# Both batches of a kv head as one unit in a decode attention block

## The chip, the cores and the metric

The kernel runs on one core of a Trainium2 chip. Five engines work side by side, each in the order of its own instructions: TensorE (PE) multiplies matrices into PSUM, VectorE (DVE), ScalarE (ACT) and GpSimd (POOL) work on elements, and SyncE (SP) issues here all transfers between device memory and SBUF. The metric is the time of one execution in device microseconds, as the median of some runs; a profile is taken of one execution of its own.

## The reference

A decode step for two sequences (B = 2, one token each): adaptive layer norm, attention over the last 4096 cached positions with 32 query heads on 8 kv heads (4 query heads share one), then a feed-forward layer, each with a gate and a residual.

```python
mod = (silu(c) @ w_mod).reshape(2, 6, 1, 512)       # shift, scale, gate, twice
h = layernorm(x) * (1 + ca) + sa
q = h @ wq                                          # 512 -> 32 heads x 128
scores = q . k[last 4096] * 128 ** -0.5             # per batch and kv head: 4 x 4096
o = softmax(scores) @ v[last 4096]
x = x + ga * (o @ wo)                               # 4096 -> 512
h = layernorm(x) * (1 + cb) + sb
out = x + gb * (silu(h @ w1) @ w2)                  # 512 -> 1792 -> 512
```

All is float32. The keys and values of the 16 pairs of kv head and batch are 2 MB each, 64 MB in all; the weights are some 30 MB.

## The kernel before, in words

**Transfers.** All big loads go through one ring of eight tiles of 128 x 4096 floats (`RING`, lines 20, 55 and 69), issued by SP in the order in which the program asks for them: `w_mod`, `wq`, keys and values, `wo`, `w1`, `w2`. A new tile takes the slot that is released first in program order, and its transfer is issued when the last reader of that slot is done. `fetch(t)` (L341) asks for the keys of step t and the values of step t-1, so that keys and values alternate.

**Steps.** A step t is one pair of kv head and batch (`seq`, L337). Keys arrive with 32 consecutive positions on each partition. `keys` (L348) turns a quarter of a key tile with VectorE's transpose of 32 x 32 blocks, so that four transposes of 128 x 1024 make `kT`. `scores` (L363) multiplies with the query, spread over a block pattern of 32 columns (`qbd`): four products over j are summed, each for four column groups cc of the array, and group cc takes the 256 columns of quarter cc of the keys. So the scores of a step are 128 x 256: four groups of 32 rows. Each float32 product is two records in the profile (two passes).

**Softmax.** `maxima` (L376) takes the maximum of each row; a product with the identity (L460) turns the 128 maxima into a row `mT`; `maxrow` (L381) reduces it to one value per query head (`mg`) and spreads it again (`mrow`); `exponentials` (L395) turns `mrow` into a bias by a product with `negscale` (`bp`, L398) and computes exponentials with the row sums. `turn` (L411) transposes them (`xp`) and spreads them over a mask (`zp`); `permute` (L423) multiplies by a small identity (`pT`) and copies the result to `ptb`.

**Values.** `weighted` (L306) multiplies the probabilities with the value tile in eight products of 512 columns, on four column groups, in two halves, and copies the sum to `ob` (L322). `collect` (L325) sums it into `o_all`, which holds the outputs of all heads for one batch in 32 rows per column group.

**Order.** The loop at L436 writes the order out by hand, and `keep_in_program_order` binds each engine to it. In iteration t VectorE turns half of the keys of t, does `maxrow` of t-1, turns the other half, does `turn` of t-1; TensorE does the scores of t, collects t-2, permutes and weights t-1. After the loop come the row sums (`rx`, `lp`, `rl`, L484 to L501), the normalisation (`on`), a product that spreads heads (`oq`, `oTn`, L505 to L512), the output product (`acc_o`, L530, and `ao`, L539), the second norm and the feed-forward layer (`hid` L570, `uT` L602, `acc_yw` L604, `acc_y` L614).

Of the kernel before, what the change touches and what calls it, by code (L numbers as in the profile page):

```python
# [13 lines left out]
P = 128  # L14
# [9 lines left out]
def adaln_block(  # L24
# [80 lines left out]
    for t, src in ((c_ch, c), (x_ch, x2)):  # L105
# [25 lines left out]
    selg = const([P, G], "selg")  # L131
    nc.vector.tensor_reduce(
        selg, id4[:, 0:16].rearrange("p (i g) -> p g i", g=G), axis=AX.X, op=ALU.add
    )

# [42 lines left out]
    rowsum = const([P, HKV, B], "rowsum")  # L178
# [48 lines left out]
    for k in range(4):  # L227
# [8 lines left out]
        if k == 0:  # L236
            mean_a, rstd_a = moments(x_ch, "a")
            xn = once.tile([P, P], F32, tag="xs", name="xn_a")
# [6 lines left out]
    h_a = once.tile([P, P], F32, tag="h", name="h_a")  # L245
# [56 lines left out]
    o_all = bank("O", "o_all")[:, : B * DH].rearrange("p (b d) -> p b d", b=B)  # L302

    o_ps = {}

    def weighted(t, vt, part):  # L306


        if part == 0:
            o_ps[t] = bank("D", f"o{t}")  # L310
        for c in range(4):
            n = 4 * part + c
            inorder(nc.tensor.matmul(  # L313
                o_ps[t][32 * c : 32 * c + 32, :],
                ptb[t % 2][:, 16 * n : 16 * n + 32],
                vt[:, 512 * n : 512 * n + 512],
                start=(part == 0),
                stop=(part == 1),
            ))
        if part == 1:  # L320
            sb_ = once.tile([P, 4 * DH], F32, tag="wide", name=f"ob{t}")
            inorder(nc.scalar.copy(sb_, o_ps[t]))  # L322
            return sb_

    def collect(t, b, h, o_sb):  # L325

        for m in range(4):
            inorder(nc.tensor.matmul(  # L328
                o_all[32 * m : 32 * m + 32, b, :],
                selh[:, m, HQ - G - G * h : 2 * HQ - G - G * h],  # L330
                o_sb[:, m * DH : (m + 1) * DH],
                start=(t == 0),
                stop=(t == NP - 1),
                skip_group_check=True,
            ))

    seq = [(h, b) for h in range(HKV) for b in range(B)]  # L337
    NP = len(seq)
    kt, vt, wot, kT = {}, {}, [], {}

    def fetch(t):  # L341

        if t < NP:
# [313 lines left out]
```

## Time and profile before

| | |
|---|---|
| median of 3 runs | 238.27 us (238.16 to 239.41) |
| the profiled execution | 237.98 us, span 236.2 us |
| transfers | 97.75 MB, mean 414 GB/s, queue 1 busy for 97.1% of the span |
| PE | 160.8 us busy (68%), 1476 products |
| PEld (weight loads) | 61.9 us (26%) |
| DVE | 118.3 us (50%), 212 instructions |
| ACT | 35.2 us (15%) |
| POOL | 9.3 us (4%) |
| mean granted clock of TensorE | 0.848 |

A row of a group names line, engine, operation, what it writes and reads, shapes and count; then its busy time, the mean of one in ns, and the idle time of its engine before it with what ended it. A row of the timeline or of the chain begins with its start in us from the start of the span and its length. A row of a window gives busy time and number of instructions of PE, PEld, DVE, ACT and POOL, then the granted clock of TensorE, the share of the transfer engines and GB/s. PE's records are pipelined: one record is longer than the distance to the next.

### The profile page before, as it was taken

What the parts mean: (1) busy time and instruction counts of PE and PEld (TensorE: products, weight loads), DVE (VectorE), ACT (ScalarE), POOL (GpSimd) and SP (SyncE); (2) the same over time, 40 slices, a digit from 0 to 9 for tenths busy, and PEclk for the clock granted to TensorE, in tenths of its full rate; (3) what the DMA queues carried; (4) which work ended last, traced back from release to release, by engine and by line L of the source; (5) the groups of instructions that cost most, each with busy time, mean ns of one, the idle gap of its engine ahead of it and who ended that gap; (6) DMA issues with size and microseconds to landing.
All of it is one profiled execution on the core that took longest, in us unless ns stands there. A gap on an engine that the chain in (4) does not pass through costs nothing.

```text
span 236.2 us, 3508 instructions
## 1 busy us (share of the span) xinstructions
PE 160.8 (68%) x1476; PEld 61.9 (26%) x1476; DVE 118.3 (50%) x212; ACT 35.2 (15%) x96; POOL 9.3 (4%) x30
## 2 busy tenths in 40 slices
PE   0193864395978777596876869659768696694843
PEld 0121111121333233231323324324223232223302
DVE  0614000658688947658476594764946742102130
ACT  2300000103022211112011120210211202003210
POOL 8400000100000000000000000000000000000000
PEclk9998577757699997978879797995997978779799
DMA  6999999999999999999999999999999999999990
GB/s 252 424 438 422 438 433 419 433 434 436 416 441 433 416 436 430 438 416 441 427 422 438 426 436 425 441 422 425 434 430 426 430 441 416 433 432 416 425 382 31
DMA packets 7607, 97.75 MB, mean 414 GB/s; under 512 B 920, under 2 KB 936, under 8 KB 1576
## 3 DMA queue, kind: packets, MB, share of 16 engines
q1 hardware_dynamic: 7592, 97.54, 97.1%
q8 instruction: 11, 0.18, 0.3%
q14 instruction: 4, 0.03, 0.0%
HBM read 97.53 MB, written 0.00 MB: 413 GB/s over the span
## 4 chain that ended last, share of the span: by engine, by line
DMA 78%; DVE 14%; PE 5%; SPq 1%; issue 0%; ACT 0%; DVEq 0%
DMA k<-in_A_k_cache_dram 41%; DMA wo<-in_A_wo_dram 15%; DMA wq<-in_A_wq_dram 13%; DVE kT L352 12%; DMA w<-in_B_w_dram 7%; DMA wm<-in_w_mod_dram 3%; PE s L368 3%; PE q L271 2%; SPq L74 1%; PE acc_y L616 0%; DVE qbd L294 0%; DVE mrow L390 0%; DVE mx L378 0%; DVE qT L280 0%; ACT qbd L294 0%
## 5 line engine op out<-in xcount | busy, mean ns | idle before, releaser
L352 DVE STREAM_TRANSPOSE kT<-k 128x1024 f32<-128x1024 f32 x64 | 75.4, 1215 | 17.0 <-DMA k<-in_A_k_cache_dram 16.9
L368 PE MATMUL s<-kT,qbd 128*32 128x256 f32 x512 | 69.2, 512 | 9.0 <-DVE kT L352 8.2
L313 PE MATMUL o<-v,ptb 128*32 128x512 f32 x256 | 35.4, 630 | 5.7 <-ACT ptb L433 5.7
L368 PEld LDWEIGHTS s<-kT,qbd 128*32 128x32 f32 x512 | 23.4, 139 | 46.0 <-DVE kT L352 29.6
L398 PE MATMUL bp<-negscale,mrow 1*128 1x1 f32 x32 | 6.6, 274 | 22.6 <-DVE mrow L390 22.6
L378 DVE TENSOR_REDUCE mx<-s 128x1 f32<-128x256 f32 x16 | 6.8, 424 | 28.7 <-PE s L368 28.7
L271 PE MATMUL q<-wq,hq_T 128*32 128x512 f32 x64 | 12.8, 944 | 9.9 <-DMA wq<-in_A_wq_dram 9.9
L322 ACT COPY ob<-o 128x512 f32<-128x512 f32 x16 | 9.4, 586 | 37.6 <-PE o L313 37.6
L398 PEld LDWEIGHTS bp<-negscale,mrow 1*128 1x128 f32 x32 | 5.3, 205 | 36.4 <-DVE mrow L390 36.4
L433 ACT COPY ptb<-pT 128x128 f32<-128x128 f32 x16 | 4.3, 266 | 64.5 <-PE pT L426 64.5
L328 PE MATMUL o_all<-ob,selh 128*32 128x128 f32 x128 | 12.6, 295 | 1.1 <-ACT ob L322 0.7
L426 PE MATMUL pT<-zp,id 128*32 128x128 f32 x128 | 13.2, 298 | 0.2 <-DVE zp L416 0.2
L280 DVE STREAM_TRANSPOSE qT<-q 128x512 f32<-128x512 f32 x2 | 1.4, 717 | 20.0 <-PE q L271 20.0
L416 DVE TENSOR_TENSOR zp<-xp,group 128x512 f32<-128x512 f32 x16 | 11.1, 692 | 0.5
L313 PEld LDWEIGHTS o<-v,ptb 128*32 128x32 f32 x256 | 7.8, 111 | 11.7 <-ACT ptb L433 10.4
L328 PEld LDWEIGHTS o_all<-ob,selh 128*32 128x32 f32 x128 | 7.5, 124 | 4.4 <-ACT ob L322 2.3
L426 PEld LDWEIGHTS pT<-zp,id 128*32 128x32 f32 x128 | 7.7, 123 | 0.9 <-issue 0.5
L402 ACT ACTIVATE pr<-s,bias 128x256 f32<-128x256 f32 x16 | 7.6, 474 | 0.7 <-ACT bias L400 0.2
L271 PEld LDWEIGHTS q<-wq,hq_T 128*32 128x32 f32 x64 | 2.3, 145 | 19.6 <-DMA wq<-in_A_wq_dram 10.9
L414 DVE STREAM_TRANSPOSE xp<-pr 128x256 f32<-128x256 f32 x16 | 6.4, 397 | 2.2 <-ACT pr L402 2.2
L532 PE MATMUL acc_o<-wo,oTn 128*32 128x512 f32 x48 | 6.9, 735 | 0.4 <-DVE oTn L510 0.4
L203 PE MATMUL mean_a<-mv_a,avg 128*128 128x1 f32 x2 | 0.6, 361 | 9.4 <-DVE mv_a L200 9.4
(126 smaller groups left out, 94.0 us busy)
## 6 DMA issues: line engine op xcount, KB each, us to landing
k<-in_A_k_cache_dram SPq DMA_DIRECT2D x16, 2048.0 KB, 33.9
v<-in_A_v_cache_dram SPq DMA_DIRECT2D x16, 2048.0 KB, 33.0
wq<-in_A_wq_dram SPq DMA_DIRECT2D x4, 2048.0 KB
wo<-in_A_wo_dram SPq DMA_DIRECT2D x4, 2048.0 KB, 35.0
wm<-in_w_mod_dram SPq DMA_DIRECT2D x4, 1536.0 KB, 10.3
w<-in_B_w_dram SPq DMA_DIRECT2D x2, 1024.0 KB, 18.7
w<-in_B_w_dram SPq DMA_DIRECT2D x1, 1792.0 KB
w<-in_B_w_dram SPq DMA_DIRECT2D x2, 896.0 KB
```

The lines of the kernel that those rows point to most:

```text
L271: nc.tensor.matmul(q_ps[n][32 * g : 32 * g + 32, :], hq_T[:, k, :], wv[:, n, g], start=(k == 0), stop=(k == 3),)
L313: inorder(nc.tensor.matmul(o_ps[t][32 * c : 32 * c + 32, :], ptb[t % 2][:, 16 * n : 16 * n + 32], vt[:, 512 * n : 512 * n + 512], start=(p ...
L322: inorder(nc.scalar.copy(sb_, o_ps[t]))
L328: inorder(nc.tensor.matmul(o_all[32 * m : 32 * m + 32, b, :], selh[:, m, HQ - G - G * h : 2 * HQ - G - G * h], o_sb[:, m * DH : (m + 1) * DH],
L352: inorder(nc.vector.transpose(kT[t][:, :, 8 * n4 : 8 * n4 + 8, :].rearrange("p j n k -> p n j k"), kt[t][:, n4 * 1024 : (n4 + 1) * 1024].r ...
L368: inorder(nc.tensor.matmul(s_ps[t][32 * cc : 32 * cc + 32, :], qbd[h // 4][:, h % 4, b, j, :], kT[t][:, j, 8 * cc : 8 * cc + 8, :], start= ...
L378: inorder(nc.vector.tensor_reduce(mx[t], s_ps[t], axis=AX.X, op=ALU.max))
L398: inorder(nc.tensor.matmul(bp[:, 0:1], mrow[t % 2], negscale, start=True, stop=True))
L402: inorder(nc.scalar.activation(pr[t].rearrange("p s k -> p (s k)"), s_ps[t], AF.Exp, bias=bias, scale=SCALE, accum_out=rowsum[:, h, b : b ...
L416: inorder(nc.vector.tensor_mul(zp, xp[:, None, :, 0:16].to_broadcast([P, 4, 8, 16]), group[:, :, None, None].to_broadcast([P, 4, 8, 16]),))
L426: inorder(nc.tensor.matmul(tp[32 * i : 32 * i + 32, :], id4, zp.rearrange("p c s x -> p (c s) x")[:, :, 4 * i : 4 * i + 4], start=True, st ...
L532: nc.tensor.matmul(acc[32 * g : 32 * g + 32, :], oTn[:, q, :], wot[q // 8][:, q % 8, :], start=(q < 4), stop=(q >= 20),)
```

## The change

One unit is now a kv head with both batches. `fetch(h)` asks for two key tiles, then two value tiles. `scores` runs once per batch on two column groups (batch 0 on rows 0 to 63 of the result, batch 1 on rows 64 to 127), each with 512 columns, into one 128 x 512 tile. Row maxima, their exchange, bias, exponentials, `turn` (now with the permutation in it) and the copy of the probabilities run once per head with tiles of twice the size: 128 x 512 scores, 128 x 1024 `zp`, 128 x 256 `pT`. `weighted` sums all sixteen products of both batches into one tile, with the probabilities of the batches kept apart by rows (`ptb` now has 32 columns per product, half of them zero); its copy `ob` and `collect` run once per head, and `collect` writes 64 rows at a time with a `selh` of twice the width. `o_all` is 128 x 128 instead of 128 x 256, and the row sums have one column per head, so that `selg`, `half` and `even` sort the batches apart at the end. Some tiles of the ends share buffers (`xn`, `h_a`, `on`, `aoT`, `hidT`). The order of an iteration is: first quarter of keys of batch 0, `turn` of the head before, the other three quarters, `weighted` of the head before, scores of batch 0, `collect` of the head before, keys and scores of batch 1, maxima and exponentials.

```diff
@@ -128,21 +128,34 @@
         rep4.rearrange("p (a r) -> p a r", a=4), id4[:, None, :].to_broadcast([P, 4, 32])
     )
     group = const([P, 4], "group")
     nc.vector.tensor_reduce(
         group, ident.rearrange("p (a r) -> p a r", r=32), axis=AX.X, op=ALU.add
     )
-    selh = const([P, 4, 2 * HQ - G], "selh")
+    half, even = const([P, B], "half"), const([P, B], "even")
+    nc.vector.tensor_reduce(
+        half, group.rearrange("p (b c) -> p b c", b=B), axis=AX.X, op=ALU.add
+    )
+    nc.vector.tensor_reduce(
+        even, group.rearrange("p (c b) -> p b c", b=B), axis=AX.X, op=ALU.add
+    )
+    selg0, selg = const([P, G], "selg0"), const([P, B, G], "selg")
+    nc.vector.tensor_reduce(
+        selg0, id4[:, 0:16].rearrange("p (i g) -> p g i", g=G), axis=AX.X, op=ALU.add
+    )
+    nc.vector.tensor_mul(
+        selg,
+        selg0[:, None, :].to_broadcast([P, B, G]),
+        half[:, :, None].to_broadcast([P, B, G]),
+    )
+    selh = const([P, 4, HQ - G + 2 * HQ], "selh")
     nc.gpsimd.memset(selh, 0.0)
     nc.vector.tensor_copy(
-        selh[:, :, HQ - G : HQ], id4[:, 0:16].rearrange("p (m g) -> p m g", g=G)
+        selh[:, :, HQ - G :].rearrange("p m (b y) -> p m b y", b=B)[:, :, :, 0:G],
+        id4.rearrange("p (b m g) -> p m b g", b=B, g=G),
     )
     quad = const([P, 4, P], "quad")
...
-    ptb = [const([P, P + 16], f"ptb{i}") for i in range(2)]
+    ptb = [const([P, 17 * 32], f"ptb{i}") for i in range(2)]
-        nc.gpsimd.memset(t[:, P:], 0.0)
+        nc.gpsimd.memset(t, 0.0)
-    rowsum = const([P, HKV, B], "rowsum")
+    rowsum = const([P, HKV], "rowsum")
...
@@ -299,168 +313,158 @@
-    o_all = bank("O", "o_all")[:, : B * DH].rearrange("p (b d) -> p b d", b=B)
...
-    seq = [(h, b) for h in range(HKV) for b in range(B)]
...
+    o_all = bank("O", "o_all")[:, :DH]
+    inorder = tc.keep_in_program_order
     kt, vt, wot, kT = {}, {}, [], {}
...
+    s_ps, mT, pr, o_sb = {}, {}, {}, {}
+    def fetch(h):
+        for b in range(B):
+            kt[h, b] = load_k(b, h)
+        for b in range(B):
+            vt[h, b] = load_v(b, h)
+    def keys(h, b, n4):
         if n4 == 0:
...
+            kT[h, b] = ktp.tile([P, 4, 32, 32], F32, tag="kT", name=f"kT{h}_{b}")
         inorder(nc.vector.transpose(
...
+            kT[h, b][:, :, 8 * n4 : 8 * n4 + 8, :].rearrange("p j n k -> p n j k"),
+            kt[h, b][:, n4 * 1024 : (n4 + 1) * 1024].rearrange("p (n j r) -> p n j r", j=4, r=32),
         ))
...
-        s_ps[t] = bank("A", f"s{t}")[:, :256]
+    def scores(h, b):
+        if b == 0:
+            s_ps[h] = bank("A", f"s{h}")
         for j in range(4):
...
+            for c in range(2):
+                r = 64 * b + 32 * c
                 inorder(nc.tensor.matmul(
...
+                    s_ps[h][r : r + 32, :],
                     qbd[h // 4][:, h % 4, b, j, :],
-                    kT[t][:, j, 8 * cc : 8 * cc + 8, :],
+                    kT[h, b][:, j, 16 * c : 16 * c + 16, :],
                     start=(j == 0),
                     stop=(j == 3),
                 ))
...
+    def maxima(h):
+        mx = work.tile([P, 1], F32, tag="mx", name=f"mx{h}")
+        inorder(nc.vector.tensor_reduce(mx, s_ps[h], axis=AX.X, op=ALU.max))
+        mT = bank("B", f"mT{h}")
+        inorder(nc.tensor.matmul(mT[0:1, :P], mx, ident, start=True, stop=True))
+        m = mrow[h % 2]
+        mg = work.tile([1, B, G], F32, tag="mg", name=f"mg{h}")
         inorder(nc.vector.tensor_reduce(
             mg,
...
+            mT[0:1, :P].rearrange("o (b c i g) -> o b g c i", b=B, c=2, g=G)[:, :, :, :, 0:4],
             axis=AX.XY,
             op=ALU.max,
         ))
         inorder(nc.vector.tensor_copy(
...
+            m.rearrange("o (b c i g) -> o b c i g", b=B, c=2, g=G)[:, :, :, 0:4, :],
+            mg[:, :, None, None, :].to_broadcast([1, B, 2, 4, G]),
         ))
...
+    def exponentials(h):
+        bp = bank("B", f"bp{h}")
+        inorder(nc.tensor.matmul(bp[:, 0:1], mrow[h % 2], negscale, start=True, stop=True))
+        bias = work.tile([P, 1], F32, tag="bias", name=f"bias{h}")
         inorder(nc.scalar.copy(bias, bp[:, 0:1]))
...
+        pr[h] = once.tile([P, 16, 32], F32, tag="pr", name=f"pr{h}")
         inorder(nc.scalar.activation(
...
+            pr[h].rearrange("p s k -> p (s k)"),
+            s_ps[h],
             AF.Exp,
             bias=bias,
             scale=SCALE,
...
+            accum_out=rowsum[:, h : h + 1],
         ))
...
+    def turn(h):
+        xp = once.tile([P, 16, 32], F32, tag="xp", name=f"xp{h}")
+        inorder(nc.vector.transpose(xp, pr[h]))
+        zp = once.tile([P, 4, 16, 16], F32, tag="zp", name=f"zp{h}")
         inorder(nc.vector.tensor_mul(
             zp,
...
+            xp[:, None, :, 0:16].to_broadcast([P, 4, 16, 16]),
+            group[:, :, None, None].to_broadcast([P, 4, 16, 16]),
         ))
...
+        tp = bank("C", f"pT{h}")[:, : 2 * P]
         for i in range(4):
             inorder(nc.tensor.matmul(
                 tp[32 * i : 32 * i + 32, :],
                 id4,
...
+                zp.rearrange("p a s x -> p (a s) x")[:, :, 4 * i : 4 * i + 4],
                 start=True,
                 stop=True,
             ))
...
+        inorder(nc.scalar.copy(
+            ptb[h % 2]
+            .rearrange("p (b y) -> p b y", b=B)[:, :, :256]
+            .rearrange("p b (w z) -> p b w z", z=32)[:, :, :, 0:16],
+            tp.rearrange("p (b w z) -> p b w z", b=B, z=16),
+        ))
+    def weighted(h):
+        o_ps = bank("D", f"o{h}")
+        for b in range(B):
+            for w in range(8):
+                c = w % 4
+                inorder(nc.tensor.matmul(
+                    o_ps[32 * c : 32 * c + 32, :],
+                    ptb[h % 2][:, 256 * b + 32 * w : 256 * b + 32 * w + 32],
+                    vt[h, b][:, 512 * w : 512 * w + 512],
+                    start=(b == 0 and w < 4),
+                    stop=(b == 1 and w >= 4),
+                ))
+        o_sb[h] = once.tile([P, 4 * DH], F32, tag="wide", name=f"ob{h}")
+        inorder(nc.scalar.copy(o_sb[h], o_ps))
+    def collect(h):
+        for m in range(4):
+            r = 64 * (m % 2)
+            inorder(nc.tensor.matmul(
+                o_all[r : r + 64, :],
+                selh[:, m, HQ - G - G * h : 3 * HQ - G - G * h],
+                o_sb[h][:, m * DH : (m + 1) * DH],
+                start=(h == 0 and m < 2),
+                stop=(h == HKV - 1 and m >= 2),
+                skip_group_check=True,
+            ))
     fetch(0)
...
+    for h in range(HKV + 1):
+        last, now = h > 0, h < HKV
         if now:
...
+            if h + 1 < HKV:
+                fetch(h + 1)
+            keys(h, 0, 0)
         if last:
...
+            turn(h - 1)
         if now:
...
+            for n4 in range(1, 4):
+                keys(h, 0, n4)
         if last:
...
+            weighted(h - 1)
         if now:
...
+            scores(h, 0)
+        if last:
+            collect(h - 1)
         if now:
...
+            for n4 in range(4):
+                keys(h, 1, n4)
+            scores(h, 1)
+            maxima(h)
+            exponentials(h)
     gaT, sbT, cbT = turned(ga, "gaT"), turned(sb, "sbT"), turned(cb1, "cbT")
     nc.vector.tensor_copy(hT[:, :, 1:32:16], sbT[:, :, 0:32:16])
...
@@ -484,24 +488,25 @@
     rx = once.tile([P, B, HKV, G], F32, tag="rx", name="rx")
     nc.vector.tensor_mul(
         rx,
-        rowsum.rearrange("p h b -> p b h")[:, :, :, None].to_broadcast([P, B, HKV, G]),
-        selg[:, None, None, :].to_broadcast([P, B, HKV, G]),
+        rowsum[:, None, :, None].to_broadcast([P, B, HKV, G]),
+        selg[:, :, None, :].to_broadcast([P, B, HKV, G]),
     )
     lp = bank("B", "lp")
+    for r in (0, 64):
+        nc.tensor.matmul(
+            lp[r : r + 64, 0:1],
+            rx.rearrange("p b h g -> p (b h g)"),
+            ones,
+            start=True,
+            stop=True,
+        )
+    rl = once.tile([P, 1], F32, tag="rl", name="rl")
+    nc.vector.reciprocal(rl, lp[:, 0:1])
+    rlb = once.tile([P, B], F32, tag="rlb", name="rlb")
+    nc.vector.tensor_scalar(rlb, even, rl, None, op0=ALU.mult)
+    on = once.tile([P, B, DH], F32, tag="xp", name="on")
     for b in range(B):
-        for m in range(4):
-            nc.tensor.matmul(
-                lp[32 * m : 32 * m + 32, b : b + 1],
-                rx[:, b].rearrange("p h g -> p (h g)"),
-                ones,
-                start=True,
-                stop=True,
-            )
-    rl = once.tile([P, B], F32, tag="rl", name="rl")
-    nc.vector.reciprocal(rl, lp[:, :B])
-    on = once.tile([P, B, DH], F32, tag="on", name="on")
-    for b in range(B):
-        nc.vector.tensor_scalar(on[:, b, :], o_all[:, b, :], rl[:, b : b + 1], None, op0=ALU.mult)
+        nc.vector.tensor_scalar(on[:, b, :], o_all, rlb[:, b : b + 1], None, op0=ALU.mult)
     oq = bank("C", "oq")[:, : B * 32]
     for j in range(4):
         nc.tensor.matmul(
```

More of the change, by code (lines that the diff above doesn't have):

```diff
@@ L297, in adaln_block @@
             )
-    o_all = bank("O", "o_all")[:, : B * DH].rearrange("p (b d) -> p b d", b=B)
[L304 to L323, printed above, removed]
@@ L432, in permute @@
             ))
-        inorder(nc.scalar.copy(ptb[t % 2][:, :P], tp))
+        inorder(nc.scalar.copy(
[18 more added lines that the diff above has]
+        inorder(nc.scalar.copy(o_sb[h], o_ps))
@@ L435, in adaln_block @@
+    def collect(h):
[9 more added lines that the diff above has]
+            ))
     fetch(0)
-    for t in range(NP + 1):
-        u, last, now = t - 1, t > 0, t < NP
+    for h in range(HKV + 1):
+        last, now = h > 0, h < HKV
```

87 lines of the change are left out of this document (4 added, 83 removed).

## The prediction

> **What bounds the kernel now.** I read the slices of the page first, then the chain of work that ended last, the issues, the groups, the timeline around one step, and the timeline of the end.
>
> ```profile
> DMA  6999999999999999999999999999999999999990
> DMA 78%; DVE 14%; PE 5%; SPq 1%; issue 0%; ACT 0%; DVEq 0%
> k<-in_A_k_cache_dram SPq DMA_DIRECT2D x16, 2048.0 KB, 33.9
> ```
>
> The transfer engines are full from the second slice to the last but one, and 78% of the chain is transfers. A key tile lands 33.9 us after its issue: the stream always has some seven tiles queued, so no compute step before its last third is felt at once.
>
> ```profile
> 97.03 2.37 DVE kT L352 x2
> ...
> 215.17 16.53 DMA w<-in_B_w_dram
> ...
> 231.75 1.06 PE acc_y L616 x24
> ```
>
> These are chain rows. Vector work that begins at a key tile's landing (97.03) recurs each step; the same row in the timeline below stands at 184.95, nine steps on. So a step of two tiles takes 87.92 / 9 = 9.77 us, a tile 4.88, and a head of four tiles 19.5. The stream ends at 231.70, with about 1 us of TensorE behind it. The kernel is bound by bytes that the change does not touch: there is hardly anything to gain, and the question is whether the compute beside the stream still fits.
>
> **The change part by part.** The prices first.
>
> ```profile
> L352 DVE STREAM_TRANSPOSE kT<-k 128x1024 f32<-128x1024 f32 x64 | 75.4, 1215 | 17.0 <-DMA k<-in_A_k_cache_dram 16.9
> L368 PE MATMUL s<-kT,qbd 128*32 128x256 f32 x512 | 69.2, 512 | 9.0 <-DVE kT L352 8.2
> L378 DVE TENSOR_REDUCE mx<-s 128x1 f32<-128x256 f32 x16 | 6.8, 424 | 28.7 <-PE s L368 28.7
> L322 ACT COPY ob<-o 128x512 f32<-128x512 f32 x16 | 9.4, 586 | 37.6 <-PE o L313 37.6
> L433 ACT COPY ptb<-pT 128x128 f32<-128x128 f32 x16 | 4.3, 266 | 64.5 <-PE pT L426 64.5
> L416 DVE TENSOR_TENSOR zp<-xp,group 128x512 f32<-128x512 f32 x16 | 11.1, 692 | 0.5
> L402 ACT ACTIVATE pr<-s,bias 128x256 f32<-128x256 f32 x16 | 7.6, 474 | 0.7 <-ACT bias L400 0.2
> L414 DVE STREAM_TRANSPOSE xp<-pr 128x256 f32<-128x256 f32 x16 | 6.4, 397 | 2.2 <-ACT pr L402 2.2
> ```
>
> Per element: vector (1215 - 397) / 768 = 1.07 ns, scalar (586 - 266) / 384 = 0.83 ns. Merged, each softmax step of 512 columns costs mx 0.69, exp 0.69, xp 0.67, zp 1.24, ptb 0.37 us once per head; per head VectorE saves some 0.7 us, which nothing on the path waits for while the stream leads.
>
> *Scores in two column groups.* This is the dear part. A set is one pass of a product on all column groups that run side by side.
>
> ```profile
> 51.12 0.20 PEld L368 LDWEIGHTS s<-kT,qbd 128*32 128x32 f32 x4 [0.23 <-issue]
> 51.54 0.20 PEld L368 LDWEIGHTS s<-kT,qbd 128*32 128x32 f32 x4 [0.23 <-issue]
> ...
> 106.44 0.27 PE L460 MATMUL mT<-ident,mx 128*1 128x128 f32 x1
> 106.55 0.27 PE L460 MATMUL mT<-ident,mx 128*1 128x128 f32 x1
> ...
> 200.26 0.20 PEld L313 LDWEIGHTS o<-v,ptb 128*32 128x32 f32 x4 [0.66 <-issue]
> 201.11 0.20 PEld L313 LDWEIGHTS o<-v,ptb 128*32 128x32 f32 x4 [0.66 <-issue]
> ...
> 210.07 0.12 PEld L532 LDWEIGHTS acc_o<-wo,oTn 128*32 128x32 f32 x4 [0.31 <-issue]
> 210.50 0.12 PEld L532 LDWEIGHTS acc_o<-wo,oTn 128*32 128x32 f32 x4 [0.31 <-issue]
> ```
>
> ```profile
> 200.00:201.00 1.00, 1.00 (x8) 0.20 (x4) 0.00 (x0) 0.00 (x0) 0.00 (x0) 0.50 1.15 492
> 210.00:211.00 1.00, 1.00 (x16) 0.31 (x12) 0.00 (x0) 0.00 (x0) 0.00 (x0) 1.00 0.92 393
> ```
>
> Four weight loads at a time are one set. Four groups of 512 columns take 0.85 us at a granted clock of 0.50 and 0.43 at 1.00; four groups of 256 take 0.42 (half clock). A product alone (mT, 128 columns) takes 0.11 between its two passes, the same time per column as in a set of four. So a set is priced by its columns, whatever the number of groups. Before, a step's scores are 32 records (512 / 16) in 8 sets of 256: 1.7 us at full clock. After, a batch has 16 records on two groups: 8 sets of 512, 3.4 us (6.8 at half clock). Per head TensorE pays 6.8 instead of 3.4, and all of the 3.4 of a batch follows its last transpose, since the second group needs the last quarter. Ends for this price: 1.7 if the idle half of the array is filled by the other batch (below), 6.8 at half clock; I take 3.4.
>
> [...]
>
> *The clock.*
>
> ```profile
> 99.77 0.38 PE L398 MATMUL bp<-negscale,mrow 1*128 1x1 f32 x2 [2.10 <-DVE mrow L390]
> ...
> 100.25:103.70 3.45, 3.38 (x22) 0.97 (x22) 2.76 (x4) 0.66 (x3) 0.00 (x0) 0.51 1.03 442
> ```
>
> After an idle gap of 2.10 us the clock was halved for 3.45 us, which costs 1.7 us of work. In the new order TensorE idles once per head, from the bias product to the permutation (3 us and more, steps 1 and 2 below), so I charge 1.7 once per head.
>
> *Collection* becomes 64 columns wide, between scores in groups of 32. The only change of width in the trace:
>
> ```profile
> 219.50 3.01 PE L573 MATMUL hid<-w,hT_b 128*32 128x448 f32 x16 [0.57 <-DVE sq L566]
> ...
> 222.44 0.59 PE L582 MATMUL var_b<-vs,mean 128*128 128x2 f32 x2
> ```
>
> The wider product began about when the narrow records ended (219.50 + 3.01 = 222.51), so a change of width waits for the array to empty. A 128-column record is 0.27 long at a pitch of 0.11: 0.16 per change, twice.
>
> *The loop per head,* counted from the end of mrow, since VectorE goes round in order:
>
> ```profile
> 119.13 0.17 DVE L384 TENSOR_REDUCE mg<-mT 1x4 f32<-1x64 f32 x1
> 119.33 0.18 DVE L390 COPY mrow<-mg 1x64 f32<-1x64 f32 x1
> ...
> 120.55 0.19 ACT L402 ACTIVATION_READ_ACCUMULATOR pr<-s,bias 128x1 f32 x1
> ...
> 184.95 2.37 DVE L352 STREAM_TRANSPOSE kT<-k 128x1024 f32<-128x1024 f32 x2 [1.41 <-DMA k<-in_A_k_cache_dram]
> ```
>
> 1. bias and exponentials: 119.51 to 120.74, plus 0.21 for 256 more elements: 1.44 (beside it one key transpose, 1.2).
> 2. xp, zp: 1.91.
> 3. zp's end to the first weighted product: 0.86 (rows 197.85 and 199.40 below), plus 0.3 to 0.45 for the doubled permutation and copy: 1.25.
> 4. weighted, 8 sets of 512: 3.4, and 1.7 for the clock: 5.1.
> 5. scores of batch 0: 3.4.
> 6. collection, 4 sets of 128 at 0.11 and two changes: 0.75.
> 7. scores of batch 1 with the record's tail: 3.6.
> 8. mx 0.69, mT 0.38, mg and mrow 0.38, four handovers of 0.05: 1.65.
>
> Sum 19.1 us against 19.5 of stream: the loop keeps up, with 0.4 to spare; the old step had idle waits for keys of 1 to 2 us in 9.77.
>
> *The ring* of eight tiles costs nothing: the first value tile of the next head takes the slot of this head's first key tile, freed 1.2 + 1.9 + 3.6 = 6.7 us after its landing and needed five tiles (24.4 us) after it. The cover is 17 us; it goes only if the loop is that late.
>
> *Set-up and small steps* cost nothing: the larger memsets and three more small vector operations come well before the query product, which waits for its weights anyway, so that 3.45 us of cover stand there. The extra factor for the row sums (one small vector step) runs while the last weighted product does.
>
> ```profile
> 23.09 3.64 PE L271 MATMUL q<-wq,hq_T 128*32 128x512 f32 x16 [3.45 <-DMA wq<-in_A_wq_dram]
> ```
>
> *The end.* The order keys, keys, values, values leaves the last key tile third from the end: it lands at 184.95 as before, and the head's first at 180.07.
>
> ```profile
> 197.85 0.69 DVE L416 TENSOR_TENSOR zp<-xp,group 128x512 f32<-128x512 f32 x1
> 199.40 3.53 PE L313 MATMUL o<-v,ptb 128*32 128x512 f32 x16 [0.38 <-ACT ptb L433]
> 206.01 0.27 DVE L510 COPY oTn<-oq 128x64 f32<-128x64 f32 x1 [1.26 <-PE oq L507]
> 206.33 6.91 PE L532 MATMUL acc_o<-wo,oTn 128*32 128x512 f32 x48 [0.36 <-DVE oTn L510]
> 215.15 1.08 PE L541 MATMUL ao<-wo,oTn 128*32 128x128 f32 x32 [1.91 <-DMA wo<-in_A_wo_dram]
> 216.27 1.06 PE L541 MATMUL ao<-wo,oTn 128*32 128x128 f32 x32
> 230.59 0.86 PE L616 MATMUL acc_y<-w,uT 128*32 128x128 f32 x24 [0.92 <-DMA w<-in_B_w_dram]
> ```
>
> The last mrow ends at 180.07 + 19.1 - 0.24 (its exponentials were ready) = 198.9. Steps 1 to 4 follow: 208.6, 208.8 with the tail. From the last weighted record (202.93) to oTn (206.28) was 3.35: oTn is at 212.1, 5.8 later than before. The output product (6.91) ends at 219.0 instead of 213.24; its successor no longer waits 1.91 for its weights but starts 3.9 late. The feed-forward chain behind it has 0.92 of waits for weights to give back. So the end moves by 3.0 us.
>
> Against the profiled execution (span 236.2, time 237.98, 0.29 under the median of 238.27): 237.98 + 3.0 = 241.0.
>
> **The rivals.** *The loop overruns.* If a second half-clock stretch falls into a head's chain, the loop takes 20.8, 1.3 over the stream; over seven heads 9 us, so 250; in every other head, with 0.4 won back in the rest, about 3, so 244. For it: the margin is 0.4. Against it: from weighted to mT TensorE has no long gap. *No change.* The two batches use different column groups, so batch 1's scores could begin at their last transpose, 1.2 + 1.9 + 3.6 + 4.9 = 11.6, instead of step 7's 13.7: 2.1 us earlier. Without the two waits for an empty array (0.3) oTn is then at 209.7, the attention output 1.5 late, and 0.9 of that is given back by the last wait for weights: 238.6. Against it: collection stands between in program order, and the row at 222.44. [...] *Faster.* Only a stream that ends sooner does it: if fewer TensorE reads or the new order of tiles raised its rate by 1%, 2.3 us less, 235.7, decided where the tail stays under its transfers. Nothing shows such a link: the DMA digits are alike in slices with busy and idle TensorE. *The stream runs dry* needs 17 us of lateness, and is part of the first rival's far end.
>
> **How the numbers follow.** End chain late, loop about keeping up (239.5 to 244): 0.56. Loop overruns (244 to 250): 0.21. No change: 0.19. Faster: 0.04. A measurement of this kernel (238.16 to 239.41) can tell about 0.5%, 1.2 us, from no change. Slower 0.77, same 0.19, faster 0.04. The predicted time is the first case's; leaving a tenth out on each side gives 238.2 to 246.5.
>
> **What would show it.** Scores groups of 512 columns with a set pitch of 0.43 at full clock and two loads per set; key transposes that still wait for key transfers in most heads; one half-clock stretch per head, in weighted; oTn near 212; an end chain that runs through acc_o, hid and uT on PE and DVE instead of the last transfer. Wrong: batch 1's scores beside batch 0's, oTn below 210, or VectorE waiting for scores instead of keys and oTn above 215.

## The result and the profile after

The changed kernel takes 246.18 us (median of 4 runs, 245.38 to 246.68) against 238.79 us before (4 runs): a ratio of 1.0306, 95% interval 1.0262 to 1.0351. The forecast was 241.0 us; the sign was right, the size was not: the loss is some 7.4 us instead of 2.7. The profiled execution has 246.29 us, a span of 244.4 us (before 236.2) and a mean granted clock of 0.839 (before 0.848).

From the page of the changed kernel: the granted clock and the transfer engines in 40 slices, and the chain that ended last by engine and by line.

```profile
PEclk9999579679569959967985995997798599589979
DMA  6999999999999999999999999999999999999700
...
PE 56%; DMA 24%; DVE 11%; ACT 4%; issue 3%
PE s L347 20%; PE o L421 20%; DMA k<-in_A_k_cache_dram 15%; DMA wq<-in_A_wq_dram 6%; DVE zp L393 4%; PE pT L400 4%; DMA wm<-in_w_mod_dram 3%; DVE xp L391 2%; ACT pr L379 2%; PE acc_o L537 2%; DVE mx L357 2%; PE o_all L435 2%; PE acc_yw L611 1%; PE hid L578 1%; ACT ptb L407 1%
```

The transfers are still full, but end two to three slices early, and the chain, 78% transfers before, is now 56% TensorE: the scores (L347) and the weighted products (L421) hold a fifth of the span each. The waits of VectorE (us in all, times, longest) say the same:

```profile
DVE mx L357 <- PE s L347: 55.2, 8, 7.5
...
DVE kT L335 <- DMA k<-in_A_k_cache_dram: 3.8, 1, 3.8
```

VectorE waits for a key transfer once in the whole run; it waits for scores 3.7 us in the first head and about 7 us in each later one. The kernel has changed its bound from the stream to the loop. The timeline gives the loop's period in the starts of the maxima, the third to sixth left out:

```profile
81.22 0.69 DVE L357 TENSOR_REDUCE mx<-s 128x1 f32<-128x512 f32 x1 [6.93 <-PE s L347]
101.40 0.69 DVE L357 TENSOR_REDUCE mx<-s 128x1 f32<-128x512 f32 x1 [7.23 <-PE s L347]
...
183.03 0.69 DVE L357 TENSOR_REDUCE mx<-s 128x1 f32<-128x512 f32 x1 [7.51 <-PE s L347]
203.50 0.69 DVE L357 TENSOR_REDUCE mx<-s 128x1 f32<-128x512 f32 x1 [7.52 <-PE s L347]
```

The mean distance is (203.50 - 81.22) / 6 = 20.38 us, where the stream needs 19.5 and the forecast had 19.1. One head from the chain, and the windows over the same stretch:

```profile
145.94 1.24 DVE zp L393
...
147.32 1.11 PE pT L400 x8
...
148.88 6.08 PE o L421 x32
154.96 3.43 PE s L347 x16
158.38 0.59 PE o_all L435 x8
158.97 3.58 PE s L347 x16
```

```profile
143.60:147.00 3.40, 0.38 (x2) 0.29 (x2) 3.04 (x4) 0.94 (x3) 0.00 (x0) 1.00 1.00 429
147.00:150.40 3.40, 2.60 (x16) 0.63 (x20) 3.40 (x4) 0.37 (x1) 0.00 (x0) 0.50 1.02 439
150.40:153.80 3.40, 3.40 (x20) 0.79 (x16) 3.40 (x4) 0.00 (x0) 0.00 (x0) 0.50 0.98 419
153.80:157.20 3.40, 3.40 (x24) 0.92 (x18) 1.28 (x2) 0.58 (x1) 0.00 (x0) 0.99 1.05 448
```

There are two stretches of half clock in the head, not one: by windows of 0.1 us the clock falls at 147.01 (0.55 in 147.0 to 147.1) and rises at 153.84 (0.81 in 153.8 to 153.9), 6.83 us or two of 3.41 later. In the 3.4 us before them TensorE is busy for 0.38 us; in the first of the two it is busy for 2.60 us, and the clock stays at 0.50 through a second, full one. The permutation (1.11) and most of the weighted products (6.08) fall into them. The two scores, 3.43 and 3.58 us, lie one behind the other with the collection between.

The end, from the timeline:

```profile
219.61 0.27 DVE L515 COPY oTn<-oq 128x64 f32<-128x64 f32 x1 [1.26 <-PE oq L512]
...
219.93 5.36 PE L537 MATMUL acc_o<-wo,oTn 128*32 128x512 f32 x48 [0.36 <-DVE oTn L515]
```

oTn ends at 219.9, 13.6 us later than before; the output product takes 5.36 us instead of 6.91, since the clock is full there (1.00 from 219.9 to 225.3, against 0.77 over the product before), and nothing behind it waits for weights any more, so that the span grows by 8.2 us only.

### The profile page after: what moved, and what is told of

Same layout as the page of the kernel before. It is cut to its first block, busy times and chain, and to the rows that moved or that the text cites. A ratio compares the mean times of both kernels' runs of the same rounds, so it can differ in the third digit from the quotient of the medians.

```text
span 244.4 us, 2546 instructions
## 1 busy us (share of the span) xinstructions
PE 165.3 (68%) x1048; PEld 47.4 (19%) x1048; DVE 114.7 (47%) x176; ACT 25.4 (10%) x56; POOL 10.3 (4%) x30
## 4 chain that ended last, share of the span: by engine, by line
PE 56%; DMA 24%; DVE 11%; ACT 4%; issue 3%
PE s L347 20%; PE o L421 20%; DMA k<-in_A_k_cache_dram 15%; DMA wq<-in_A_wq_dram 6%; DVE zp L393 4%; PE pT L400 4%; DMA wm<-in_w_mod_dram 3%; DVE xp L391 2%; ACT pr L379 2%; PE acc_o L537 2%; DVE mx L357 2%; PE o_all L435 2%; PE acc_yw L611 1%; PE hid L578 1%; ACT ptb L407 1%
## 5 line engine op out<-in xcount | busy, mean ns | idle before, releaser
L347 PE MATMUL s<-kT,qbd 128*32 128x512 f32 x256 | 60.6, 604 | 3.8 <-DVE kT L335 3.7
L421 PE MATMUL o<-v,ptb 128*32 128x512 f32 x256 | 47.8, 914 | 3.9 <-ACT ptb L407 3.9
L357 DVE TENSOR_REDUCE mx<-s 128x1 f32<-128x512 f32 x8 | 5.5, 691 | 55.2 <-PE s L347 55.2
L400 PE MATMUL pT<-zp,id 128*32 128x256 f32 x64 | 8.6, 630 | 26.3 <-DVE zp L393 26.3
L347 PEld LDWEIGHTS s<-kT,qbd 128*32 128x32 f32 x256 | 14.2, 111 | 43.0 <-issue 36.4
L421 PEld LDWEIGHTS o<-v,ptb 128*32 128x32 f32 x256 | 10.4, 159 | 41.0 <-issue 30.1
L393 DVE TENSOR_TENSOR zp<-xp,group 128x1024 f32<-128x1024 f32 x8 | 9.8, 1225 | 0.2
L391 DVE STREAM_TRANSPOSE xp<-pr 128x512 f32<-128x512 f32 x8 | 5.7, 706 | 3.3 <-ACT pr L379 3.3
L400 PEld LDWEIGHTS pT<-zp,id 128*32 128x32 f32 x64 | 1.8, 140 | 26.8 <-issue 25.9
L435 PE MATMUL o_all<-ob,selh 128*64 128x128 f32 x64 | 5.3, 285 | 0.7 <-ACT ob L429 0.7
L379 ACT ACTIVATE pr<-s,bias 128x512 f32<-128x512 f32 x8 | 5.5, 687 | 0.2
## 6 DMA issues: line engine op xcount, KB each, us to landing
wo<-in_A_wo_dram SPq DMA_DIRECT2D x4, 2048.0 KB, 20.5
```

The lines of the kernel that those rows point to most:

```text
L347: inorder(nc.tensor.matmul(s_ps[h][r : r + 32, :], qbd[h // 4][:, h % 4, b, j, :], kT[h, b][:, j, 16 * c : 16 * c + 16, :], start=(j == 0) ...
L357: inorder(nc.vector.tensor_reduce(mx, s_ps[h], axis=AX.X, op=ALU.max))
L379: inorder(nc.scalar.activation(pr[h].rearrange("p s k -> p (s k)"), s_ps[h], AF.Exp, bias=bias, scale=SCALE, accum_out=rowsum[:, h : h + 1],))
L391: inorder(nc.vector.transpose(xp, pr[h]))
L393: inorder(nc.vector.tensor_mul(zp, xp[:, None, :, 0:16].to_broadcast([P, 4, 16, 16]), group[:, :, None, None].to_broadcast([P, 4, 16, 16]),))
L400: inorder(nc.tensor.matmul(tp[32 * i : 32 * i + 32, :], id4, zp.rearrange("p a s x -> p (a s) x")[:, :, 4 * i : 4 * i + 4], start=True, st ...
```

## The experiments

The theory: per head the loop costs about a microsecond more than the stream, by two things that cost TensorE's chain 2 to 3 us each, the scores in sequence and two stretches of half clock. The rivals: the order of the loads and the ring; the collection; a clock that has nothing to do with the gap. Each ratio below is to runs of the kernel before that were taken beside the experiment; their median is 238.28 us, and 238.96 us for the kernel with the whole collection in 32 columns and the one with one product more in the chain.

**Half of the score sum left out.**

```diff
-        for j in range(4):
+        for j in range(2):
...
-                    stop=(j == 3),
+                    stop=(j == 1),
```

> The changed kernel, whose scores sum only two of the four terms of each product (half of the score sum is left out, so that a batch's scores are 4 sets of 512 columns instead of 8, the TensorE time that they had before the change). Theory (the loop of a head overran the stream because of the scores' doubled time plus a second half-clock stretch): 3.4 us less per head at full clock takes the loop from 20.4 us to about 17 us, below the 19.5 us of stream; VectorE waits for keys again and no longer for scores, distances of the maxima follow the stream at 19.5 us, and the time falls to 238.5 to 240.5 us. If the half-clock stretches alone make the 20.4 us (a loop locked to them, whatever work is in it), the time stays at 244 to 246 us. If the cause lies in the order of loads or the ring of tiles, nothing changes: 246 us.

Measured: 237.12 us, ratio to before 0.9944 (0.9922 to 0.9966). The waits and two rows of the timeline:

```profile
DVE kT L335 <- DMA k<-in_A_k_cache_dram: 25.2, 7, 4.2
```

```profile
77.08 0.69 DVE L357 TENSOR_REDUCE mx<-s 128x1 f32<-128x512 f32 x1 [2.91 <-PE s L347]
...
193.45 0.69 DVE L357 TENSOR_REDUCE mx<-s 128x1 f32<-128x512 f32 x1 [2.60 <-PE s L347]
```

VectorE waits for keys in seven heads again, and the period, (193.45 - 77.08) / 6 = 19.40 us, is the stream's. The time is even below the 238.5 us expected. So the stretches alone don't make 20.4 us (the mean granted clock is 0.795 here, lower than in the changed kernel), and the loads are not at fault: with 3.4 us less TensorE work per head the whole loss is gone.

**Only the order of the loads, in the kernel before.**

```diff
-        if t < NP:
-            kt[t] = load_k(seq[t][1], seq[t][0])
-        if t > 0:
-            vt[t - 1] = load_v(seq[t - 1][1], seq[t - 1][0])
+        if t % 2 == 0 and t < NP:
+            for i in (t, t + 1):
+                kt[i] = load_k(seq[i][1], seq[i][0])
+            for i in (t, t + 1):
+                vt[i] = load_v(seq[i][1], seq[i][0])
...
-            fetch(t + 1)
+            fetch(t + 2)
```

> The kernel before the change, with only the order of its loads changed to that of the changed kernel: keys, keys, values, values for each head. Theory (the loss lies in TensorE's chain, not in the loads): no change, 238 to 239.5 us. If the new order of loads or the time at which tiles come free in the ring of eight holds the stream up: slower by 2 to 7 us, with gaps in the transfers' busy share.

Measured: 238.53 us, ratio 1.0009 (0.9994 to 1.0023). The new order of the tiles costs nothing.

**The collection behind the maxima.**

```diff
             scores(h, 0)
-        if last:
-            collect(h - 1)
         if now:
             for n4 in range(4):
                 keys(h, 1, n4)
             scores(h, 1)
             maxima(h)
+        if last:
+            collect(h - 1)
+        if now:
             exponentials(h)
```

> The changed kernel with the collection of the head before moved from between the two batches' scores to behind the maxima of the second, so that nothing stands between the scores of column groups 0 and 1 and those of groups 2 and 3 in TensorE's order. If the two batches' scores can run side by side when nothing is between them (the forecast's rival of no change): the second batch's scores begin while the first's run, 2 to 3.4 us less per head on the chain, the loop is under the stream's 19.5 us and the time is 238.5 to 240.5 us. If groups in TensorE's order pass one behind another, or the second batch's key transposes end too late for it: only the collection's 0.6 us leaves the chain of a head, 19.8 to 20.4 us per head, 243.5 to 246 us.

Measured: 237.35 us, ratio 0.9950 (0.9926 to 0.9975). From the timeline, and from the waits:

```profile
165.28 5.10 PE L421 MATMUL o<-v,ptb 128*32 128x512 f32 x32 [0.48 <-ACT ptb L407]
170.21 5.36 PE L347 MATMUL s<-kT,qbd 128*32 128x512 f32 x32
```

```profile
DVE kT L335 <- DMA k<-in_A_k_cache_dram: 18.2, 7, 3.1
```

The two scores are one group of 32 records, 5.36 us long, where scores, collection and scores take 3.43 + 0.59 + 3.58 = 7.60 in the changed kernel. So the batches' scores can run beside each other, and a collection of 0.6 us between them prevented it: moving it is worth 2.2 us per head. This version is also half a per cent faster than the kernel before.

**Why the collection keeps them apart.** It has four products of 64 columns, two on the column groups 0 and 1, which batch 0's scores occupy, and two on the groups 2 and 3, which are free. Two kernels leave only those for the free groups between the scores, two products of 64 columns in the first and four of 32 in the second, and move the others, 64 columns wide in both, behind the maxima. `collect` gets the products and their width as arguments.

```diff
-            collect(h - 1)
+            collect(h - 1, (1, 3))        # second kernel: collect(h - 1, (1, 3), 32)
...
             maxima(h)
+        if last:
+            collect(h - 1, (0, 2))
...
```

> The changed kernel with the collection split: its two 64-column products on column groups 2 and 3 (the odd ones) stay between the two batches' scores, its two on groups 0 and 1 (the even ones) move behind the maxima. The batch 0 scores run on groups 0 and 1, so nothing between the scores needs a group that is occupied. Theory A (TensorE takes products in order, and the collection's first product waited for the occupied groups 0 and 1 with all of batch 1's scores behind it): now nothing waits, batch 1's scores run beside batch 0's, 5.4 us for both instead of 7.8, and the time is 237 to 238.5 us as with the collection moved whole. Theory B (a change of the group width from 32 to 64 columns waits until the array is empty): the scores of the two batches still follow each other, 3.4 + 0.5 + 3.5 us, the loop is 20 us or a little more, 243 to 246 us.

> The same split collection, but the odd products between the two batches' scores are made 32 columns wide (four products on groups 2 and 3 instead of two of 64 columns), the width of the scores themselves; the even ones, 64 wide, stay behind the maxima. Theory A (order and occupied groups): as with 64 columns, both 237 to 238.5 us. Theory B (the change of width empties the array): here nothing changes width between the scores, so batch 1's scores run beside batch 0's and the time is 237 to 238.5 us, while the 64-wide one stays at 243 to 246 us. If any other product between the scores serialises them, both stay at 243 to 246 us.

Measured: 246.33 us with 64 columns, ratio 1.0341 (1.0308 to 1.0374); 237.13 us with 32, ratio 0.9966 (0.9935 to 0.9996). One head of the timeline of the first, then of the second:

```profile
154.75 3.60 PE L347 MATMUL s<-kT,qbd 128*32 128x512 f32 x16
158.28 0.65 PE L435 MATMUL o_all<-ob,selh 128*64 128x128 f32 x4
158.87 3.63 PE L347 MATMUL s<-kT,qbd 128*32 128x512 f32 x16
```

```profile
170.18 2.31 PE L347 MATMUL s<-kT,qbd 128*32 128x512 f32 x10
171.91 0.63 PE L437 MATMUL o_all<-ob,selh 128*32 128x128 f32 x8
172.33 3.65 PE L347 MATMUL s<-kT,qbd 128*32 128x512 f32 x22
```

With 64 columns the collection starts when batch 0's scores are through (154.75 + 3.60 = 158.35), though its groups were free while they ran and its input `ob` was ready at about 155.5 (the weighted products end at 154.93, the copy takes 0.59), and batch 1's scores follow it. With 32 columns it starts 1.73 us after the first scores and amid them, and all three together take 172.33 + 3.65 - 170.18 = 5.80 us. The width of these products alone makes 9 us of difference (246.33 against 237.13).

**The whole collection between the scores, in 32 columns.**

```diff
-            r = 64 * (m % 2)
-            inorder(nc.tensor.matmul(
-                o_all[r : r + 64, :],
-                selh[:, m, HQ - G - G * h : 3 * HQ - G - G * h],
+            for i in (0, 32):
+                r = 64 * (m % 2) + i
+                a = HQ - G - G * h + i
+                inorder(nc.tensor.matmul(
+                    o_all[r : r + 32, :],
+                    selh[:, m, a : a + 32],
...
```

> The changed kernel with the collection in its place between the batches' scores but in eight products of 32 columns, as before the change, instead of four of 64; nothing else differs. The order of the products over the column groups is 0, 1, 2, 3, so the first ones need groups that batch 0's scores occupy. If only the change of the group width serialises the scores: batch 1's scores begin before batch 0's end, maxima follow the stream at 19.5 us, 237 to 238.5 us. If a product that waits for its occupied group also holds back the products behind it (TensorE takes them in order): the scores of batch 1 still start behind batch 0's, save the width changes' 0.3 us, so 20.2 to 20.5 us per head and 244 to 246.5 us.

Measured: 238.95 us, ratio 1.0006 (0.9970 to 1.0042), with times from 237.37 to 240.39. It lies between the numbers of the two theories. From the timeline of the profiled run, which is one of the quicker ones (237.63 us):

```profile
150.72 3.17 PE L347 MATMUL s<-kT,qbd 128*32 128x512 f32 x14
153.31 0.41 PE L437 MATMUL o_all<-ob,selh 128*32 128x128 f32 x4
153.72 0.60 PE L347 MATMUL s<-kT,qbd 128*32 128x512 f32 x2
...
154.84 3.17 PE L347 MATMUL s<-kT,qbd 128*32 128x512 f32 x14
```

Here the products on occupied groups do hold back the scores of batch 1: from first to last it is 154.84 + 3.17 - 150.72 = 7.29 us, not 5.4. But that is 0.46 us less than in the changed kernel, by the same reckoning on its rows (158.97 + 3.58 - 154.96 = 7.59 in the chain, 158.90 + 3.63 - 154.78 = 7.75 in the timeline), and it brings the period to 19.7 us on average: about 19.95 in five heads, and 18.45 in one. So order and occupied groups serialise too, and most of the loss hangs on the last half microsecond.

**Products in the gap.** Three products of 512 columns, read by nobody, right behind the bias product; then one.

```diff
         inorder(nc.scalar.copy(bias, bp[:, 0:1]))
+        wp = bank("B", f"wp{h}")
+        for _ in range(3):                # second kernel: range(1)
+            inorder(nc.tensor.matmul(
+                wp[0:32, :],
+                qbd[h // 4][:, h % 4, 0, 0, :],
+                kT[h, 1][:, 0, 0:16, :],
+                start=True,
+                stop=True,
+            ))
```

> The changed kernel with three added products of 512 columns (a result that nobody reads) right behind the bias product of each head, 2.6 us at the half clock or 1.3 us at the full one, in the gap of about 3 us in which TensorE waits for exponentials and zp. Theory (the half clock that follows this gap costs about 3 us of each head's chain): with the gap filled the granted clock stays near 1.0 through the permutation and the weighted products (weighted 3.5 us instead of 6.08, the permutation 0.6 instead of 1.08), the loop falls to 17 to 18 us, the stream paces again, 238.5 to 240.5 us. If the fill is too short to keep the clock, the loop stays at 20.4 us: 246 us. If the clock follows something else than idleness (power, the number of columns), more work makes it lower: 246 to 248 us.

> The changed kernel with one added product of 512 columns behind the bias product of each head, where the kernel with three (237.31 us) had the clock at 0.917 instead of 0.839. One product is 0.43 us at the full clock, 0.85 us at the half one; TensorE still stands idle for more than half of the gap. Theory (the clock falls when TensorE is busy for too small a part of one fixed stretch of about 3.4 us): one product is not enough, the half-clock stretches stay, the loop stays at about 20.4 us per head, 244 to 247 us. If any work in the gap keeps the clock: 237 to 238.5 us, like the three products.

Measured: 237.31 us with three, ratio 0.9966 (0.9939 to 0.9992); 245.67 us with one, ratio 1.0313 (1.0259 to 1.0368). With three, one head of the timeline and its window:

```profile
160.14 2.76 PE L380 MATMUL wp<-kT,qbd 128*32 128x512 f32 x6
163.68 0.64 PE L409 MATMUL pT<-zp,id 128*32 128x256 f32 x8 [0.78 <-DVE zp L402]
164.81 3.64 PE L430 MATMUL o<-v,ptb 128*32 128x512 f32 x32 [0.49 <-ACT ptb L416]
168.26 3.60 PE L347 MATMUL s<-kT,qbd 128*32 128x512 f32 x16
```

```profile
163.10:166.50 3.40, 2.33 (x24) 0.71 (x28) 3.40 (x4) 0.37 (x1) 0.00 (x0) 1.00 0.99 424
```

More work made the kernel 9 us faster. The permutation takes 0.64 instead of 1.08 us, the weighted products 168.26 - 164.81 = 3.45 instead of 6.08: the two stretches of half clock cost 0.45 + 2.6 = 3.1 us per head. (A product is two records of 0.43 us at the full clock, so the three take 2.6 us, 2.76 in the row above with the tail of the last; the expectation counted half of that.) Only every second head is like this one. In the others VectorE waits over 2 us for keys (2.23 to 2.32), `zp` comes late, one stretch of half clock remains (0.50 from 183.60 to 187.00 in one of them), and the weighted products take 4.56 to 5.38 us; the mean period, (196.82 - 80.42) / 6 = 19.40 us, is the stream's. Scores and collection are as in the changed kernel, still in sequence. So neither cause makes the loss without the other, as far as these kernels go.

With one product, the windows and the period:

```profile
144.30:147.70 3.40, 1.32 (x4) 0.43 (x4) 2.98 (x4) 0.94 (x3) 0.00 (x0) 1.00 1.00 429
147.70:151.10 3.40, 2.73 (x16) 0.60 (x20) 3.40 (x4) 0.37 (x1) 0.00 (x0) 0.50 0.99 424
151.10:154.50 3.40, 3.40 (x20) 0.79 (x16) 3.40 (x4) 0.00 (x0) 0.00 (x0) 0.50 1.06 453
```

Here 1.32 us of work in a stretch of 3.4 did not keep the clock: it is 0.50 in the next two. The maxima stand at 81.31 and 204.17, (204.17 - 81.31) / 6 = 20.48 us apart.

```profile
81.31 0.69 DVE L357 TENSOR_REDUCE mx<-s 128x1 f32<-128x512 f32 x1 [7.53 <-PE s L347]
...
204.17 0.69 DVE L357 TENSOR_REDUCE mx<-s 128x1 f32<-128x512 f32 x1 [7.47 <-PE s L347]
```

**One product more in the chain.**

```diff
             scores(h, 0)
+        if last and now:
+            wp = bank("B", f"wp{h}")
+            inorder(nc.tensor.matmul(
+                wp[0:32, :],
+                qbd[h // 4][:, h % 4, 0, 0, :],
+                kT[h, 0][:, 0, 0:16, :],
+                start=True,
+                stop=True,
+            ))
         if last:
             collect(h - 1)
```

> The changed kernel with one added product of 512 columns between batch 0's scores and the collection, on column group 0, in the middle of each head's chain of products: 0.43 us more per head at the full clock. In the changed kernel the heads follow each other at 20.46 to 20.48 us, six stretches of 3.413 us, and the half-clock stretches begin with the permutation. If the distance of the heads is locked to the stretches (a longer chain begins later in its first half-clock stretch and so pays less half clock), the added 0.43 us costs nothing: maxima still 20.48 us apart, 245.5 to 246.8 us. If the costs simply add: 20.9 us per head, 3 us more in all, 248.5 to 250 us.

Measured: 245.65 us, ratio 1.0293 (1.0260 to 1.0325): not slower than the changed kernel. From the chain, and from the timeline:

```profile
150.91 5.32 PE o L421 x32
156.22 3.43 PE s L347 x16
159.65 0.85 PE wp L462 x2
```

```profile
82.28 0.69 DVE L357 TENSOR_REDUCE mx<-s 128x1 f32<-128x512 f32 x1 [8.07 <-PE s L347]
103.02 0.69 DVE L357 TENSOR_REDUCE mx<-s 128x1 f32<-128x512 f32 x1 [7.73 <-PE s L347]
...
205.68 0.69 DVE L357 TENSOR_REDUCE mx<-s 128x1 f32<-128x512 f32 x1 [7.48 <-PE s L347]
```

The product costs 0.85 us on the chain, for both its records (the expectation counted one), and the weighted products beside it shrink from 6.08 to 5.32: the head comes later in its first half-clock stretch and pays less of it. Here the permutation begins at 149.33, 1.8 us after the clock fell (at 147.5), and in the changed kernel at 147.32, 0.3 us after (at 147.0). The period falls from 20.74 us at first to 20.49 at the end, while in the changed kernel it rose from 20.18 to 20.47.

**Both remedies.** The late collection and the three products in one kernel.

> Collection moved behind the maxima and three added products in the gap, both in one kernel: each alone took the loop below the stream's 19.5 us per head (237.35 and 237.31 us). Theory (with the loop below the stream, the stream's end and what follows the last weights set the time): no addition of the two gains, 236.5 to 237.5 us, VectorE waits longer for keys (over 25 us in all). If the loop still held the stream up in either: lower than both by over 1 us, 235 to 236.3 us.

Measured: 237.39 us, ratio 0.9944 (0.9919 to 0.9968). The two gains don't add: once the loop is under the stream, the stream sets the time. VectorE's waits for keys are 20.5 us in all, less than expected.

The five kernels that bring the loop below the stream with room to spare (237.12, 237.35, 237.31, 237.13 and 237.39 us) lie about 1 us below the kernel before, 0.3 to 0.6% by their ratios, and below the least that was expected of the first three (238.5). The load order alone did not give that (238.53); which other part of the change does was not tried.

## Why the prediction was wrong, point by point

- *Bound by the stream, hardly anything to gain.* Right: no median here is under 237.1 us. But the changed kernel left that bound, where the forecast had the loop keep up with the stream.
- *Scores in two column groups: priced by columns, 3.4 us a batch.* Right: 3.43 and 3.58 us against 3.4 and 3.6.
- *The clock: "so I charge 1.7 once per head".* This is the step that failed, and a term of the sum that was too small. The row it came from showed one stretch of half clock after a gap of 2.10 us. In the new order the gap is 3.16 us, the first half-clock stretch begins as it ends (at 147.0) and holds only 2.60 us of work, and a second one follows: 3.1 us instead of 1.7. One row was not enough: between 100 and 210 us the kernel before has nine single stretches and, after a gap of 2.65 us, this double one:

```profile
158.32:161.73 3.41, 3.24 (x20) 1.44 (x24) 3.35 (x5) 0.72 (x3) 0.00 (x0) 0.50 0.99 423
161.73:165.15 3.42, 3.42 (x38) 1.73 (x30) 0.42 (x1) 0.00 (x0) 0.00 (x0) 0.50 1.04 446
```

- *Collection: 0.75, with two changes of width.* The time is nearly right (0.59), and so were both arguments against "no change": that a change of width waits for the array to empty (with 64 columns the collection began at 158.28, where batch 0's scores end at 158.35; with 32 it began 1.73 us after they did) and that the collection stands between in program order (the whole collection in 32 columns still holds the scores apart, 7.29 us for both against 5.36). The sum had the scores one behind the other, so this was no error of the forecast. But it was a choice of the order, not a price of the two groups: moving the collection gave 2.2 us per head, where the rival had put 2.1. (Steps 1 to 6 add up to 13.85 us, not to the 13.7 in that rival.)
- *The loop per head: 19.1, "0.4 to spare".* Steps 1, 2, 5, 7 and 8 came within 0.1 us, as far as one head's rows show; step 3 took 1.70 (from 145.94 + 1.24 to 148.88) instead of 1.25, weighted 6.08 instead of 5.1, collection 0.16 less. The sum is 20.4. The rival "loop overruns" (a second half-clock stretch in a head's chain, 20.8 us and 250) is what happened, in every head; it was given 0.21. The measured 246.18 us is in its ground (244 to 250), and just inside the stated range (238.2 to 246.5) only because that range reached into it. The argument against it, that TensorE has no long gap from weighted to mT, was true and beside the point: the second stretch needs no second gap. Of the signs named for the forecast, one half-clock stretch per head and keys awaited in most heads did not come.
- *Ring, set-up, small steps at nothing.* Right as far as it shows: transfers stay full until the last slices, and the load order alone changes nothing.
- *The end.* The last mrow was forecast at 198.9; the last maximum begins at 203.50 and mrow ends about 1.6 later, 6.2 late. The last head's steps cost 1.6 more, so oTn is at 219.9 instead of 212.1. The chain behind it was 2.6 us shorter than forecast (244.4 - 219.9 = 24.5 against 239.2 - 212.1 = 27.1), chiefly as the output product ran at the full clock (5.36 instead of 6.91). 7.8 - 2.6 = 5.2 us is the error of the forecast.
- *What would show it wrong* was named: VectorE waiting for scores instead of keys, and oTn above 215.

## What to carry to other kernels

When a change makes a loop of compute about as long as the stream it hides under, the margin is the forecast: here 0.4 us was claimed, a term was 1.4 us too small, and every head paid the difference. Don't take the price of a half clock from one row: see how often it is two stretches in the trace, and work the loop out for both. And put nothing of another column width between products that could share the array: here the same products a few lines later (237.35 us against 246.18), or half of them there and the others made narrower (237.13), gave back the whole loss.

## What was not expected of the hardware

*The loop locks to the clock's stretches.* The granted clock of the kernel before and of the changed one changes only on a grid of 3.413 us (in the latter the half clock sets in at 85.57 and again at 208.45, 36 steps later): from 17.3 us on there, and from 15.0 on in the kernel before, each window of such a grid has 1.00 or 0.50, none a value between. Six steps are 20.48 us. By windows of 0.1 us, the half clock of the changed kernel sets in at 85.5, 106.0, 126.5, 147.0, 167.4, 187.9 and 208.4 us, 20.5 us apart from the second head on, while the heads only draw near to this distance. The periods of three kernels go there from below (20.18 to 20.47), from above (20.74 to 20.49) and stay there (20.48 in the kernel with one product in the gap). In this state a product of 0.85 us more did not show (245.65 us against 246.18), and the loss is the same for different causes: the four kernels in it have 245.65 to 246.33 us. The kernel with the whole collection in 32 columns, 0.46 us shorter, is not held: its maxima are 18.45 to 20.02 us apart from the second on. That the lock, and not only the shorter chain, makes its 7 us is not shown.

*How much work keeps the clock.* By the windows, a stretch of 3.4 us with 0.38, 1.32 or 1.20 us of work was followed by half clock, one with 2.33 us was not. In the rows above and below, a half-clock stretch with 2.60 or 2.73 us of work was followed by a second, and one with 2.91 us was not:

```profile
180.20:183.60 3.40, 1.20 (x10) 0.16 (x8) 3.37 (x4) 0.00 (x0) 0.00 (x0) 1.00 0.98 419
183.60:187.00 3.40, 2.91 (x20) 0.79 (x20) 3.40 (x4) 0.37 (x1) 0.00 (x0) 0.50 1.02 439
...
187.00:190.40 3.40, 3.40 (x28) 0.90 (x22) 3.40 (x4) 0.58 (x1) 0.00 (x0) 1.00 1.01 426
```

These are windows of the kernel with three products, in another head than the one above. They give no threshold: in the kernel before, a half-clock stretch with 3.24 us of work was followed by a second one (the rows at 158.32 above). A full-clock stretch with 1.75 us of work in the same kernel (202.69 to 206.10) was followed by half clock, and one with 1.50 us (212.93 to 216.34) was not. What decides, beside the busy time, stays open. The changed loop falls to the half clock in each head: 3.1 us in 20.4, enough to turn a change of no effect into 3% (ratio 1.0306, and 0.9966 with three products in the gap).
